# Attention, weight decoding and weight splitting without GpSimd arithmetic; phi in one VectorE instruction less a subtraction

## The chip, the cores and the metric

The kernel runs on one core of one Trainium2 chip. The metric is device microseconds of one execution, and a version's time is the median of its runs; less is better. The core's engines work beside each other, each through its own queue in order: TensorE (PE, with its weight loads as PEld), VectorE (DVE), ScalarE (ACT), GpSimd (POOL) and SyncE (SP, which issues the DMAs here).

## What is computed

Attention over 4 batches, 8 heads, 576 positions and 64 features, followed by two feed-forward layers of 2304 tokens, 512 columns and 2048 hidden columns. All inputs come as float64 words for the weights and float32 for the rest.

```python
scores = scale * q @ k.T, causal;  a = softmax(scores);  local = a @ v
phi(x) = where(x > 0, x, exp(x) - 1) + 1
mem_out = (phi(q) @ M_prev) / (phi(q) @ z_prev + 1e-6)
x = g * mem_out + (1 - g) * local          # g = sigmoid(beta), one number a head
h = x @ w_in;   x = gate(h) @ w_out        # first layer:  0, ((h + 1) ** 2) / 4 or h
h = x @ w2_in;  x = max(0.01 * h, h) @ w2_out
```

## The kernel before

Each float32 product is made of three products of float32r parts: a number is split into a high part (a cast) and a low part (the number less its high part). **Weights** take three steps. `load_raw` brings the float64 words of half a slot (128 hidden columns of W_in, or of W_out) as [128, 512, 2] integers. `decode_a` and `decode_b` make float32 of them: a ScalarE copy (L122), four VectorE instructions (L123, L127, L129, L130) and the addition L132 on GpSimd. `split` makes the two parts: a ScalarE copy (L188) and the subtraction L189 on GpSimd. There are 64 decoded halves in all, and 80 splits.

**Attention** goes by 16 units, each a pair of heads. `prep` splits and transposes q and k and makes phi: VectorE's minimum L297, GpSimd's q less the minimum (L298), ScalarE's exponential (L299), GpSimd's sum (L302), VectorE's row sum with z (L304 to L308) and GpSimd's product with the norm (L309). `scores` runs over five tiles of queries: matmuls, the masked minimum L360, the exponential L363, one over the sum (L365 to L367), and the product of e with it. That product is on VectorE (L370) for the first head of the first four tiles, and on GpSimd (L372) for the five others of a unit. `turn_a`, `turn_b` and `values` transpose e and multiply by v.

**Feed-forward.** Each layer is done in two halves of the hidden columns, each half over nine chunks of 256 tokens. A first-layer chunk has eight steps; a step is 12 matmuls (L527 to L529), ScalarE's L534 and L535, VectorE's L536 to L538, and, two steps later (`LAG`), 12 matmuls that use the result (L548 to L550). In the second layer a step has two slots: L576 to L578 for 24 matmuls, ScalarE's L581, VectorE's L582 to L586, ScalarE's L727, VectorE's L708, and 21 matmuls (L599 to L601) two such steps later. `finish2` adds up products on VectorE; when a chunk is visited the second time, L632 on GpSimd adds the first visit's part.

When one half of a layer gives way to the next, new weights have to be split into the places of the old ones. This happens at three **switches**: within the first layer (515 to 548 us of the trace), from the first to the second layer (740 to 783 us), and within the second layer (950 to 1000 us). The next weights are decoded ahead of that, at the steps in the tables `FETCH` and `HALVES`.

**Order.** While attention runs (the first 450 us), a scheduler sets each engine's order by its own estimate of times; the first-layer steps are interleaved by `target`. From then on every engine but SP goes in the order in which the code is written. An engine that waits holds all that stands behind it on its queue.

Of the kernel before, what the change touches and what calls it, by code (L numbers as in the profile page):

```python
# [25 lines left out]
# (layer, half of the hidden columns, chunks of tokens)  # L26
# [6 lines left out]
# whose quotients by the sums the vector engine works out: (tile of queries, head)  # L33
ON_DVE = {(i, 0) for i in range(4)}
# the tile of queries behind whose scores phi is transposed and v loaded
# [3 lines left out]
# tiles of scores between two of the first segment's slots, before the first, and from decoding to splitting  # L39
BOOT, BOOT0, DELAY = 2.0, 12.0, 1.0  # L40
# steps at which the next segment's weights are fetched
# [10 lines left out]
def attn_moe_moe_kernel(ctx, tc, q, k, v, m_prev, z_prev, beta, w1i, w1o, w2i, w2o, out):  # L52
# [17 lines left out]
    # scores are kept negated, so the mask is +1e9 and the row maximum is a minimum  # L70
# [4 lines left out]
    # both heads' last 64 queries stand one above the other  # L75
# [16 lines left out]
    # tiles with parts that are set once  # L92
# [5 lines left out]
    for s in range(2):  # L98
        # the last 64 queries: a head's own columns, zeros for the other head's
        ql = att.tile([128, 2, 128], F32R, bufs=1, name=f"ql{s}")  # L100
        nc.vector.tensor_copy(ql.rearrange("p a t -> p (a t)"), mask[:, 0:256])
        ql_t.append(ql)
        vn = att.tile([128, NKT, 2, D], F32, bufs=1, name=f"vn{s}")
        vn_t.append(vn)
# [21 lines left out]
    def decode_b(lo, dst, a, r):  # L126
# [5 lines left out]
        nc.gpsimd.tensor_tensor(dst, a.bitcast(F32), r, ALU.add)  # L132
# [3 lines left out]
    def l2_pool():  # L136
        """the second layer's tiles, in the attention's room"""
# [5 lines left out]
    def load_raw(seg, f, x):  # L143
        """a slot's float64 words of W_in (x = 0) or W_out (x = 1): [128, 512, 2]"""
# [18 lines left out]
    def fetch_halves(seg, halves):  # L163
        """weights as float32 in SBUF; two steps a half, the float64 words are loaded two halves ahead"""
# [22 lines left out]
    def split(dst, src):  # L187
        nc.scalar.activation(dst[:, 0], src, AF.Copy)  # L188
        nc.gpsimd.tensor_tensor(dst[:, 1], src, as_r(dst[:, 0]), ALU.subtract)  # L189
# [6 lines left out]
    def split_out(seg, p):  # L196
        """the second layer: W_out of two slots as the four blocks B and the combinations
        T1 = B12 - B11, T2 = B22 - T1, T3 = B22 - B12, T4 = T2 - B21; T1 takes the place of B12"""
# [20 lines left out]
    # a unit of attention: a pair of heads  # L219
# [21 lines left out]
    def prep(u):  # L241
        """-q/8 and k of a pair of heads, transposed, high part above low part, and phi of q over its norm"""
# [44 lines left out]
        # k with its parts exchanged, for the cross terms  # L287
# [5 lines left out]
        # phi(q) = exp(min(q, 0)) + (q - min(q, 0))  # L293
# [4 lines left out]
        nc.gpsimd.tensor_tensor(ph, qn, fe, ALU.subtract)  # L298
        nc.scalar.activation(fe, fe, AF.Exp)  # L299
        if u + 1 < len(UNITS):  # L300
            load_rows(q, qn, u + 1)
        nc.gpsimd.tensor_tensor(ph, ph, fe, ALU.add)  # L302
# [6 lines left out]
        nc.gpsimd.tensor_tensor(ph, ph, nn.unsqueeze(3).broadcast_to([128, NKT, 2, D]), ALU.mult)  # L309
# [18 lines left out]
    def scores(u, i):  # L328
        """exp of the scores less their maximum, over its sum and times the gate; of the last 64 rows, those of both
        heads at once"""  # L330
# [37 lines left out]
        for h, e in enumerate(es):  # L368
            if (i, h) in ON_DVE:
                nc.vector.tensor_scalar(out=e[:, 0:w], in0=e[:, 0:w], scalar1=ls[:, h:h + 1], scalar2=None, op0=ALU.mult)  # L370
            else:
                nc.gpsimd.tensor_tensor(e[:, 0:w], e[:, 0:w], ls[:, h:h + 1].broadcast_to([128, w]), ALU.mult)  # L372
        e_t[u, i] = es

    # the outputs of a pair of heads, features by queries: the first 256 queries, then the other 320
# [15 lines left out]
    def turn_b(u, j):  # L391
        """of the keys' tile j: first head: queries' tiles 2, 3 and 4; second head: 4, 2 and 3"""
# [23 lines left out]
    def values(u, half):  # L416
# [6 lines left out]
        for j, pt in enumerate(pts):  # L423
# [5 lines left out]
            else:  # L429
                # queries' tile 4 of the second head lies behind the first head's columns  # L430
# [11 lines left out]
    def attention_steps():  # L442
        """yields the number of tiles of 128 queries that are scored"""
# [65 lines left out]
    def load_prev(n):  # L509
        """what a chunk's first visit left"""  # L510
# [9 lines left out]
    def mm_h(n, f):  # L520
# [12 lines left out]
        # where h < 1: max(h / 2 + 1 / 2, 0) ** 2, at most 1; above: h  # L533
# [7 lines left out]
    def mm_y(n, f, yp, gg):  # L541
        w = slots[f, 1]
        gh, gl = gg
        for et in range(4):
            wh, wl = w[:, 0, 128 * et:128 * et + 128], w[:, 1, 128 * et:128 * et + 128]
            o = yp[et // 2][:, et % 2]
            # the two accumulators of a bank are one group
# [18 lines left out]
    def mm_h2(n, p):  # L566
        """lhsT blocks: 0 A21, 1 A11, 2 A22, 3 A12, 4 S1 = A21 + A22, 5 S2 = S1 - A11, 6 S3 = A11 - A21, 7 S4 = A12 - S2;
        A1. are the later 128 tokens of the chunk, A.1 the first slot"""
# [22 lines left out]
    def mm_y2(n, p, yp, gg):  # L591
        wa, wb, ex = slots["out", p]
        gh, gl = gg[1:]
        # P1 = A11 B11, P6 = S2 T2, P7 = S3 T3, P5 = S1 T1, P2 = A12 B21, P3 = S4 B22, P4 = A22 T4
        products = ((0, wa, 0), (4, ex, 0), (5, ex, 256), (3, wa, 256), (2, wb, 0), (6, wb, 256), (1, ex, 512))
        for i, (a, w, c) in enumerate(products):
            # the two accumulators of a bank are one group
# [5 lines left out]
    def finish2(n, yp):  # L603
# [15 lines left out]
        if last:  # L619
            # nothing runs beside it: the first visit's part goes into the summands that are ready early  # L620
# [182 lines left out]
```

## Time and profile before

| | us |
|---|---|
| median of three runs (lowest, highest) | 1178.47 (1175.47, 1181.21) |
| span of the profiled execution | 1174.2 |
| PE busy | 1085.9 (92%) |
| DVE busy | 949.5 (81%) |
| ACT busy | 583.5 (50%) |
| POOL busy | 389.0 (33%) |

The median is 4.3 us above the profiled execution's span; that execution's whole time is not listed apart. A matmul's busy time is longer than the distance to the next one's start, so that a PE that reads as fully busy may still not issue at its highest rate: the number of matmuls in a stretch tells more. The share of an engine over the whole span is a mean over stages that differ; the table of stretches below separates them. PEclk is the clock that TensorE was granted, as a share of the full one.

### The profile page before, as it was taken

What the parts mean: (1) busy time and instruction counts of PE and PEld (TensorE: products, weight loads), DVE (VectorE), ACT (ScalarE), POOL (GpSimd) and SP (SyncE); (2) the same over time, 40 slices, a digit from 0 to 9 for tenths busy, and PEclk for the clock granted to TensorE, in tenths of its full rate; (3) what the DMA queues carried; (4) which work ended last, traced back from release to release, by engine and by line L of the source; (5) the groups of instructions that cost most, each with busy time, mean ns of one, the idle gap of its engine ahead of it and who ended that gap; (6) DMA issues with size and microseconds to landing.
All of it is one profiled execution on the core that took longest, in us unless ns stands there. A gap on an engine that the chain in (4) does not pass through costs nothing.

```text
span 1174.2 us, 22682 instructions
## 1 busy us (share of the span) xinstructions
PE 1085.9 (92%) x8520; PEld 1023.8 (87%) x8520; DVE 949.5 (81%) x2125; ACT 583.5 (50%) x1314; POOL 389.0 (33%) x300
## 2 busy tenths in 40 slices
PE   5777687999999999997999999989999997999997
PEld 4544476999989889997999999889999997999997
DVE  5789999777677775998688787899999888876776
ACT  5755564766667765454333333444444444433332
POOL 3456666433343431236001111742121256211211
PEclk9866698999999999999999999989999998999999
DMA  5345444434334321432233433123232210121121
GB/s 146 93 97 144 139 128 132 111 80 125 102 76 116 77 60 60 142 108 72 80 119 122 130 114 121 55 72 127 90 103 96 91 37 37 63 100 55 66 79 55
DMA packets 122174, 112.11 MB, mean 95 GB/s; under 512 B 67280, under 2 KB 100048, under 8 KB 122064
## 3 DMA queue, kind: packets, MB, share of 16 engines
q1 hardware_dynamic: 122064, 110.66, 31.5%
q8 instruction: 67, 1.10, 0.4%
q14 instruction: 43, 0.35, 0.1%
HBM read 77.60 MB, written 23.59 MB: 86 GB/s over the span
## 4 chain that ended last, share of the span: by engine, by line
PE 68%; DVE 20%; issue 5%; POOL 3%; DMA 1%; ACT 1%; SPq 0%; DVEq 0%; POOLq 0%; ACTq 0%
PE A L576 5%; PE A L577 5%; PE A L578 5%; PE y L549 3%; PE A L527 3%; PE A L528 3%; PE A L529 3%; PE y L550 3%; PE A L348 3%; PE y L548 3%; PE y L601 3%; PE y L600 2%; PE y L599 2%; DVE gh L537 2%; DVE da L127 2%
## 5 line engine op out<-in xcount | busy, mean ns | idle before, releaser
L576 PE MATMUL A<-xh,i 128*128 128x256 f32 x576 | 163.7, 284 | 0.0
L577 PE MATMUL A<-xl,i 128*128 128x256 f32 x576 | 163.7, 284 | 0.0
L578 PE MATMUL A<-xh,i 128*128 128x256 f32 x576 | 163.5, 284 | 0.0
L132 POOL TENSOR_TENSOR w32b<-da,dr 128x512 f32<-128x512 f32 x36 | 55.2, 1532 | 282.2 <-DVE dr L130 269.3
L727 ACT ACTIVATE gh<-g 128x896 fp32r<-128x896 f32 x72 | 68.6, 953 | 155.9 <-DVE g L586 93.8
L363 ACT ACTIVATE e<-e,mx 128x128 f32<-128x128 f32 (+2 forms) x144 | 84.3, 586 | 76.3 <-DVE mx L360 72.7
L534 ACT ACTIVATE g<-A 128x256 f32<-128x256 f32 x98 | 37.6, 384 | 167.3 <-PE A L529 154.5
L372 POOL TENSOR_TENSOR e<-e,ls 128x128 f32<-128x128 f32 (+4 forms) x80 | 76.8, 960 | 123.6 <-DVE ls L367 59.3
L549 PE MATMUL y<-gl,o 128*128 128x256 f32 x384 | 112.2, 294 | 3.9 <-DVE gl L538 3.7
L548 PE MATMUL y<-gh,o 128*128 128x256 f32 x384 | 107.8, 289 | 5.7 <-DVE gh L537 5.7
L528 PE MATMUL A<-xl,i 128*128 128x256 f32 x392 | 111.3, 284 | 1.0 <-DVE xl L506 1.0
L527 PE MATMUL A<-xh,i 128*128 128x256 f32 x392 | 111.5, 284 | 0.0
L576 PEld LDWEIGHTS A<-xh,i 128*128 128x128 f32 x576 | 111.4, 193 | 0.0
L577 PEld LDWEIGHTS A<-xl,i 128*128 128x128 f32 x576 | 111.3, 193 | 0.0
L578 PEld LDWEIGHTS A<-xh,i 128*128 128x128 f32 x576 | 111.2, 193 | 0.0
L529 PE MATMUL A<-xh,i 128*128 128x256 f32 x392 | 111.2, 284 | 0.0
L550 PE MATMUL y<-gh,o 128*128 128x256 f32 x384 | 111.0, 290 | 0.0
L708 DVE TENSOR_TENSOR gl<-g,gh 128x896 fp32r<-128x896 f32 x72 | 87.8, 1219 | 19.8 <-ACT gh L727 19.8
L537 DVE CAST gh<-g 128x256 fp32r<-128x256 f32 x144 | 80.0, 556 | 19.6 <-PE y L550 7.9
L360 DVE CUSTOM_DVE_ANT_0 e<-A,mask 128x128 f32<-128x128 f32 (+4 forms) x126 | 59.6, 479 | 39.4 <-PE A L348 38.3
L549 PEld LDWEIGHTS y<-gl,o 128*128 128x128 f32 x384 | 74.7, 195 | 5.8 <-DVE gl L538 5.3
L548 PEld LDWEIGHTS y<-gh,o 128*128 128x128 f32 x384 | 72.9, 193 | 7.1 <-DVE gh L537 6.8
(289 smaller groups left out, 3736.8 us busy)
## 6 DMA issues: line engine op xcount, KB each, us to landing
raw<-in_moe_w_in_dram SPq DMA_DIRECT2D x32, 512.0 KB, 3.7
raw<-in_moe_w_out_dram SPq DMA_DIRECT2D x32, 512.0 KB, 3.3
qk<-qk SPq DMA_DIRECT2D x64, 144.0 KB, 2.4
xf<-y_d SPq DMA_DIRECT2D x18, 512.0 KB, 3.6
xf<-x_d SPq DMA_DIRECT2D x12, 512.0 KB, 4.0
yp_d<-ys SPq DMA_DIRECT2D x18, 256.0 KB, 2.3
xf<-yp_d SPq DMA_DIRECT2D x9, 512.0 KB, 3.2
y_d<-ys SPq DMA_DIRECT2D x18, 256.0 KB, 2.2
```

The lines of the kernel that those rows point to most:

```text
L363: nc.scalar.activation(e[:, 0:w], e[:, 0:w], AF.Exp, bias=mx, scale=-1.0, accum_out=ls[:, h:h + 1])
L527: nc.tensor.matmul(hp, wh, xh[:, ct], start=(ct == 0), stop=False)
L528: nc.tensor.matmul(hp, wh, xl[:, ct], start=False, stop=False)
L529: nc.tensor.matmul(hp, wl, xh[:, ct], start=False, stop=(ct == 3))
L537: nc.vector.tensor_copy(gh, g)
L548: nc.tensor.matmul(o, wh, gh, start=(f == 0 and et % 2 == 0), stop=False)
L549: nc.tensor.matmul(o, wh, gl, start=False, stop=False)
L550: nc.tensor.matmul(o, wl, gh, start=False, stop=(f == NSLOT - 1 and et % 2 == 1))
L576: nc.tensor.matmul(o, wh, xh[:, ct], start=(s == 0 and ct == 0), stop=False)
L577: nc.tensor.matmul(o, wh, xl[:, ct], start=False, stop=False)
L578: nc.tensor.matmul(o, wl, xh[:, ct], start=False, stop=(s == 1 and ct == 3))
L708: nc.vector.tensor_tensor(gl, g[:, 1:8], as_r(gh), ALU.subtract)
```

## The change

All GpSimd arithmetic of attention, decoding and splitting becomes VectorE arithmetic: L132 and L189 change their engine, L372 becomes the same per-row product as L370, and L309 changes its engine. Phi is now exp(min(q, 0)) + max(q, 0): L298 goes, and L302 becomes one VectorE instruction that takes the maximum of q and 0 and adds the exponential; it stands right behind the exponential. GpSimd keeps the fills at the start and the 16 additions of L632. Comments went too, so lines of the changed kernel have numbers up to six less.

```diff
-        nc.gpsimd.tensor_tensor(dst, a.bitcast(F32), r, ALU.add)
+        nc.vector.tensor_tensor(dst, a.bitcast(F32), r, ALU.add)
...
         nc.scalar.activation(dst[:, 0], src, AF.Copy)
-        nc.gpsimd.tensor_tensor(dst[:, 1], src, as_r(dst[:, 0]), ALU.subtract)
+        nc.vector.tensor_tensor(dst[:, 1], src, as_r(dst[:, 0]), ALU.subtract)
...
         nc.vector.tensor_scalar(out=fe, in0=qn, scalar1=0.0, scalar2=None, op0=ALU.min)
-        nc.gpsimd.tensor_tensor(ph, qn, fe, ALU.subtract)
         nc.scalar.activation(fe, fe, AF.Exp)
+        nc.vector.scalar_tensor_tensor(out=ph, in0=qn, scalar=0.0, in1=fe, op0=ALU.max, op1=ALU.add)
         if u + 1 < len(UNITS):
             load_rows(q, qn, u + 1)
-        nc.gpsimd.tensor_tensor(ph, ph, fe, ALU.add)
...
-        nc.gpsimd.tensor_tensor(ph, ph, nn.unsqueeze(3).broadcast_to([128, NKT, 2, D]), ALU.mult)
+        nc.vector.tensor_tensor(ph, ph, nn.unsqueeze(3).broadcast_to([128, NKT, 2, D]), ALU.mult)
...
-            if (i, h) in ON_DVE:
-                nc.vector.tensor_scalar(out=e[:, 0:w], in0=e[:, 0:w], scalar1=ls[:, h:h + 1], scalar2=None, op0=ALU.mult)
-            else:
-                nc.gpsimd.tensor_tensor(e[:, 0:w], e[:, 0:w], ls[:, h:h + 1].broadcast_to([128, w]), ALU.mult)
+            nc.vector.tensor_scalar(out=e[:, 0:w], in0=e[:, 0:w], scalar1=ls[:, h:h + 1], scalar2=None, op0=ALU.mult)
```

**First switch.** VectorE's queue in a step of the first layer at the first switch. Here da, dr and raw are decoding, g, gh and gl a step's result, i_ and o_ the split weights. Before:

```order
L123 TENSOR_SCALAR da<-raw 128x512
L127 SCALAR_TENSOR_TENSOR da<-w32b,da 128x512
L129 TENSOR_SCALAR dr<-da 128x512
L130 SCALAR_TENSOR_TENSOR dr<-raw,dr 128x512
L536 SCALAR_TENSOR_TENSOR g<-A,g 128x256
L537 CAST gh<-g 128x256
L538 TENSOR_TENSOR gl<-g,gh 128x256
```

The same step in the changed kernel:

```order
L187 TENSOR_TENSOR o_6954<-w_5026,o_6954 128x512
L187 TENSOR_TENSOR i_6957<-w_5464,i_6957 128x512
L121 TENSOR_SCALAR da<-raw 128x512
L125 SCALAR_TENSOR_TENSOR da<-w32b,da 128x512
L127 TENSOR_SCALAR dr<-da 128x512
L128 SCALAR_TENSOR_TENSOR dr<-raw,dr 128x512
L130 TENSOR_TENSOR w32b<-da,dr 128x512
L530 SCALAR_TENSOR_TENSOR g<-A,g 128x256
L531 CAST gh<-g 128x256
L532 TENSOR_TENSOR gl<-g,gh 128x256
```

Two split subtractions and the decoding's addition now stand ahead of the step's own three instructions.

**Third switch.** VectorE's queue in a step of the second layer at the third switch. Before, from the combinations of W_out to the next step's first instruction:

```order
L203 TENSOR_TENSOR g<-w32b 128x256
L204 TENSOR_TENSOR t<-w32b,g 128x256
L205 TENSOR_TENSOR t<-w32b 128x256
L206 TENSOR_TENSOR t<-t,w32b 128x256
L708 TENSOR_TENSOR gl_12406<-g_12398,gh_12405 128x896
L582 TENSOR_TENSOR g_12480<-A,g_12480 128x512
```

The same stretch of the changed kernel:

```order
L201 TENSOR_TENSOR g<-w32b 128x256
L202 TENSOR_TENSOR t<-w32b,g 128x256
L203 TENSOR_TENSOR t<-w32b 128x256
L204 TENSOR_TENSOR t<-t,w32b 128x256
L187 TENSOR_TENSOR wa<-w32b,wa 128x256
L187 TENSOR_TENSOR wb<-w32b,wb 128x512
L187 TENSOR_TENSOR i_12426<-w32b,i_12426 128x512
L187 TENSOR_TENSOR i_12429<-w32b,i_12429 128x512
L702 TENSOR_TENSOR gl_12390<-g_12382,gh_12389 128x896
L187 TENSOR_TENSOR wa<-g,wa 128x256
L187 TENSOR_TENSOR ex<-t,ex 128x768
L576 TENSOR_TENSOR g_12464<-A,g_12464 128x512
```

Four split subtractions now stand ahead of the low part gl, and two more behind it.

## Rows read from the trace of the kernel before

**Rows 1.** Stretches: us; busy us (xcount) of PE, PEld, DVE, ACT, POOL; clock; DMA.
```profile
70.00:212.00 142.00, 104.18 (x610) 81.48 (x612) 138.98 (x299) 82.03 (x214) 93.22 (x69) 0.76 0.47 132
212.00:515.00 303.00, 300.68 (x2474) 277.52 (x2469) 225.75 (x666) 192.66 (x526) 100.21 (x86) 1.00 0.35 96
515.00:548.00 33.00, 26.42 (x185) 25.13 (x186) 31.32 (x40) 16.47 (x34) 22.50 (x16) 0.90 0.26 80
548.00:740.00 192.00, 192.00 (x1602) 192.00 (x1602) 148.59 (x297) 65.63 (x157) 25.90 (x20) 1.00 0.34 110
740.00:783.00 43.00, 36.59 (x264) 35.58 (x263) 38.51 (x54) 20.41 (x39) 29.85 (x22) 0.88 0.16 54
783.00:950.00 167.00, 166.04 (x1384) 165.84 (x1383) 153.98 (x314) 75.09 (x105) 34.26 (x18) 1.00 0.29 97
950.00:1000.00 50.00, 41.94 (x331) 41.34 (x330) 41.72 (x68) 23.06 (x40) 30.62 (x23) 0.93 0.11 40
```

**Rows 2.** Timeline near 512 us: start, us, engine, line, what [idle before].
```profile
512.36 1.28 POOL L132 TENSOR_TENSOR w32b<-da,dr 128x512 f32<-128x512 f32 x1 [6.13 <-DVE dr L130]
...
512.66 1.14 DVE L537 CAST gh<-g 128x256 fp32r<-128x256 f32 x1
```

**Rows 3.** Three VectorE lines over the run: nanoseconds min/median/max.
```profile
L370 DVE TENSOR_SCALAR e<-e,ls x64: 220/420/1434, 18.0 to 443.2; 128x128 f32<-128x128 f32 x16, 128x256 f32<-128x256 f32 x16, 128x384 f32<-128x384 f32 x16, 128x512 f32<-128x512 f32 x16
...
L537 DVE CAST gh<-g x144: 223/294/1619, 148.5 to 759.3; 128x256 fp32r<-128x256 f32 x144
...
L365 DVE TENSOR_SCALAR ls<-ls x80: 134/156/1502, 16.1 to 446.9; 128x2 f32<-128x2 f32 x64, 128x1 f32<-128x1 f32 x16
```

**Rows 4.** VectorE by line, 70 to 212 us: busy us, mean ns | idle before.
```profile
L127 DVE SCALAR_TENSOR_TENSOR da<-w,da 128x512 int32<-128x512 int32 x19 | 19.7, 1036 | 0.1
L370 DVE TENSOR_SCALAR e<-e,ls 128x256 f32<-128x256 f32 (+3 forms) x16 | 16.9, 1059 | 0.0
L130 DVE SCALAR_TENSOR_TENSOR dr<-raw,dr 128x512 f32<-128x512 uint32 x20 | 15.9, 794 | 0.0
...
L123 DVE TENSOR_SCALAR da<-raw 128x512 int32<-128x512 int32 x19 | 13.6, 714 | 2.1 <-DMA raw<-in_moe_w_in_dram 2.1
L129 DVE TENSOR_SCALAR dr<-da 128x512 int32<-128x512 int32 x19 | 12.6, 664 | 0.1
L365 DVE TENSOR_SCALAR ls<-ls 128x2 f32<-128x2 f32 (+1 forms) x20 | 7.6, 378 | 0.0
...
L537 DVE CAST gh<-g 128x256 fp32r<-128x256 f32 x8 | 6.7, 834 | 0.0
```

**Rows 5.** VectorE by line, 548 to 740 us, where GpSimd is mostly idle.
```profile
L130 DVE SCALAR_TENSOR_TENSOR dr<-raw,dr 128x512 f32<-128x512 uint32 x16 | 11.1, 692 | 0.6
...
L127 DVE SCALAR_TENSOR_TENSOR da<-w32b,da 128x512 int32<-128x512 int32 x12 | 8.3, 693 | 1.2
L129 DVE TENSOR_SCALAR dr<-da 128x512 int32<-128x512 int32 x16 | 6.8, 427 | 0.5
L123 DVE TENSOR_SCALAR da<-raw 128x512 int32<-128x512 int32 x16 | 6.7, 420 | 0.0
```

**Rows 6.** GpSimd by line, 70 to 212 us.
```profile
L132 POOL TENSOR_TENSOR w<-da,dr 128x512 f32<-128x512 f32 x20 | 28.8, 1442 | 36.9 <-DVE ls L367 19.2 <-DVE dr L130 10.8 <-DVE ls L366 5.6
L372 POOL TENSOR_TENSOR e<-e,ls 128x256 f32<-128x256 f32 (+4 forms) x21 | 21.9, 1046 | 10.5 <-DVE ls L367 8.7 <-DVE ls L366 0.8 <-DVE ls L365 0.4
```

**Rows 7.** Line L189 alone in the stretches: us, GpSimd busy (instructions), clock, DMA.
```profile
70.00:212.00 142.00, 24.54 (x16) 0.76 0.47 132
515.00:548.00 33.00, 18.78 (x13) 0.90 0.26 80
740.00:783.00 43.00, 29.85 (x22) 0.88 0.16 54
950.00:1000.00 50.00, 30.62 (x23) 0.93 0.11 40
```

**Rows 8.** ScalarE's copy in a split, over the run.
```profile
L188 ACT ACTIVATE i<-w32b 128x512 fp32r<-128x512 f32 x17 | 9.9, 615 | 0.0
```

More of the change, by code (lines that the diff above doesn't have):

```diff
@@ L32 @@
 NW, RAWB, SPB, EB, GB = 4, 2, 2, (2, 2, 2, 2, 1), 2
-ON_DVE = {(i, 0) for i in range(4)}
 PHI, VL = 3, 0
```

## The prediction

> **What bounds the kernel now.** The table of stretches comes first, since an engine's share over the whole span mixes stages [rows 1]. In the second layer's quiet stretch PE issues 1384 matmuls in 167 us, in the first layer's 1602 in 192 us: 0.12 us each, with PE busy throughout. No work on another engine can shorten such a stretch. From 212 to 515 us, where attention ends beside the first layer, PE is busy for 300.7 of 303 us, which I read the same way. Four stretches are different. From 70 to 212 us VectorE is busy 139.0 of 142 us and PE 104, at a granted clock of 0.76: VectorE sets the pace. At the three switches PE issues 185, 264 and 331 matmuls, which at 0.12 us need 22.2, 31.7 and 39.7 us; the stretches last 33, 43 and 50 us. So 10.8, 11.3 and 10.3 us are lost there, 32.4 in all, and VectorE is busy 31.3 of 33, 38.5 of 43 and 41.7 of 50 us. Part of PE's loss is its clock, at 0.88 to 0.93 in these stretches: it fell after PE had waited and comes back with its work.
>
> Next I ask whether VectorE really works in that time. The cast L537 takes 0.29 us in the median and up to 1.62 [rows 3]. In the timeline one of 1.14 us starts 0.30 us after a GpSimd addition of 1.28 us and outlasts it by 0.16 us [rows 2]. Line by line the same instruction is long where GpSimd is busy (93 of 142 us) and short where it is mostly idle (26 of 192 us): L127 takes 1036 against 693 ns, L123 714 against 420, L129 664 against 427 [rows 1, 4, 5]. I read this as VectorE being held while GpSimd works. A good part of its busy time is waiting, and goes with GpSimd's instructions.
>
> **The change part by part: prices.** A moved addition or split subtraction of 512 columns does what L130 does, with two operands of that width: 0.69 us [rows 5]. A moved product with e is an L370: 0.42 us in the median of its four widths [rows 3]; the shape of 576 columns is a little wider. Phi's two instructions are 640 wide; no undisturbed row has this shape, so 0.69 scaled by the columns, an estimate of 0.87 us, lies between 0.69 and twice that. L298 costs nothing any more. The second layer's splits have 256, 512 and 768 columns; I price all at 0.69 us, which is dear for the narrow ones, more numerous than the wide.
>
> **Attention, 70 to 212 us.** Moved onto VectorE: 20 additions L132 and 16 subtractions L189, 36 times 0.69 = 24.8 us; 21 products L372, 21 times 0.42 = 8.8 us [rows 6, 7]. At five products a unit these are four units, with two phi instructions each: 8 times 0.87 = 7.0 us. Sum 40.6 us. Taken away, as count times (mean here less the undisturbed value): L127 19 x 343 ns = 6.5 us, L123 19 x 294 = 5.6, L129 19 x 237 = 4.5, L130 20 x 102 = 2.0, L370 16 x 639 = 10.2, L365 20 x 222 = 4.4, L537 8 x 540 = 4.3 [rows 3 to 5]. Sum 37.5 us from 121 of the stretch's 299 instructions. If the other 178 lost nothing, the stretch grows by 3 us. If a fifth of them, 36, lost the same 0.31 us each, 11 us more go and the stretch falls by 8. I take 5 us less: the splitting of q and k, phi and L367 are among the 178 and have the same kind of operands. Phi's chain also becomes shorter by two GpSimd instructions, but the start before 70 us hangs on loads and matmuls too; I count nothing there.
>
> **First switch.** VectorE has 40 instructions in 31.3 us, 0.78 us each; the same work from 548 to 740 us has 297 in 148.6, 0.50 each [rows 1]. The difference, 11.3 us, is a floor for what was waiting, since 0.50 holds some too. Added: 13 split subtractions and, by GpSimd's 16 instructions, 3 additions: 16 x 0.69 = 11.0 us [rows 1, 7]. VectorE would need 31.0 us. The gain lies between 2 us, if it still sets the pace and the floor is all, and 10.8 us, if PE does. A step's result is wanted two steps later, 24 matmuls or 2.9 us each, so VectorE may lag without stopping PE. I take 8 us, nearer to PE's end.
>
> **Second and third switch.** Second: 54 instructions at 0.71 us against 0.50 give 11.5 us; 22 subtractions add at most 15.2; VectorE 42.2 of 43 us; gain between 0.8 and 11.3 us, taken as 6. Third: 68 at 0.61 us against 0.49 (154.0 us by 314, 783 to 950 us) give 8.3 us; 23 subtractions add at most 15.9; VectorE 49.3 of 50; gain between 0.7 and 10.3 us, taken as 6 [rows 1, 7]. I go to the middle because the price is a ceiling, and because the delay of two steps covers a burst.
>
> **Where I cost it at nothing.** From 212 to 515, 548 to 740 and 783 to 950 us PE's matmuls hide VectorE. This cover is thin in the last: 154.0 of 167 us busy, and GpSimd's 18 instructions there become 12.4 us. Were nothing freed, VectorE would stand at 166.4 of 167 us, and bursts would cost some us. From 212 to 515 us 77 us are free, against GpSimd's 86 instructions of at most 0.87 us: 75 us. The additions L632, still on GpSimd, go on holding VectorE behind 1000 us, as now.
>
> **Waits that the move adds.** A split subtraction waits for ScalarE's copy of 0.62 us [rows 8]. On GpSimd this held up nobody; on VectorE the step's own g, gh and gl, or the second layer's gl, stand behind it, and PE wants those. At the first switch two copies a step are due behind the previous step's matmuls, while VectorE still decodes; mostly they will be done.
>
> **Sum.** 5 + 8 + 6 + 6 = 25 us off the span of 1174.2: 1149. The median shown is 4.3 us above that span, so the time is 1153 us.
>
> One rule speaks against the change. The Trainium skill, "Perfetto Trace Analysis", section "Optimizing Scalar/DVE Operations", says that where VectorE is saturated, moving work from it to ScalarE or even GpSimd may make sense, and adds that GpSimd shares an SBUF port with VectorE, so that moving between these two might not help. By its first half alone the moved 40.6 us would all be paid for (fourth rival); the 1036 against 693 ns of L127 agree with the second half. The Trainium skill, "SBUF — State Buffer", section "Who interferes with whom", has a VectorE instruction with two SBUF inputs, or in a two-port mode, blocked for the whole of a GpSimd instruction that reads SBUF; the timeline's 1.14 us cast agrees, and by that rule all excess goes.
>
> **The rivals.** *Deeper:* PE ends up the bound at all three switches and attention falls by its 8 us: 32.4 + 8 = 40 us, so 1138. For it: VectorE's floor is low. Against: VectorE's sum stays above PE's need in each switch. *No gain at the switches:* the floors are right, VectorE stays the bound there, 2.0 + 0.8 + 0.7 = 3.5 us, and attention loses 5 or gains 3: 1170 to 1178; 1173 in the middle. For it: all three sums come out within 2 us of the stretch. Against: the delay of two steps. *Slower by ScalarE's copies:* 74 of the split subtractions lie in the four stretches [rows 7]. If each held VectorE for a whole copy, 74 x 0.62 = 46 us, the time is 1153 + 46 = 1199. It cancels the gain from 0.34 us a piece, and shows as slower by over 0.5% (about 6 us, what a measurement here can tell from no change) from 0.42. For it: in the second layer ScalarE has four copies in a row, and VectorE only four short instructions to pass the time. Against: ScalarE is busy only 16.5 of 33, 20.4 of 43 and 23.1 of 50 us [rows 1]. *Slower, nothing is freed:* the long times are not GpSimd's doing. Then 40.6 + 11.0 + 15.2 + 15.9 = 83 us come onto an engine with 3.0 + 1.7 + 4.5 + 8.3 = 17.5 us free in these stretches: 66 us more, 1244. Against: every line in rows 4 and 5.
>
> **How the numbers follow.** Forecast 0.64 (1153, its own range 1143 to 1164), deeper 0.12 (1138), no gain at the switches 0.13 (1173), copies 0.07 (1199), nothing freed 0.04 (1244). Faster by over 0.5% (below 1172.6): 0.64 + 0.12 and half of the third case, 0.82. Within 0.5%: its other half, 0.07. Slower: 0.11. The range runs from 1136, a little past the deeper case, to 1175, past the third's middle; it leaves out some 0.05 below and 0.15 above.
>
> **What would show it.** Right: L127 near 0.69, L123 and L129 near 0.42, L370 near 0.42 us with no long ones, L537 at 0.29 throughout; VectorE's busy time about the same in total; the three switches shorter by 6 to 8 us each, the quiet stretches as long as now. Wrong: VectorE idle ahead of L187 with ScalarE's L186 as releaser (copies); long VectorE instructions with GpSimd idle (nothing freed); PE waiting for VectorE's gl between 783 and 950 us (thin cover).

## The result and the profile after

The changed kernel takes 1142.1 us (median of four runs, 1139.99 to 1144.17) against 1177.7 us (four runs, 1175.47 to 1181.21): a ratio of 0.9696, 95% interval 0.9673 to 0.9719, so 35.6 us less. The forecast was 1153 us, and its range 1136 to 1175. The sign, the mechanism and that range held. The narrower range of 1143 to 1164, to which the prediction gave a chance of 0.64, was missed by 1 us, because one of the terms of the 25 us, attention, was much too small.

To see where the 35 us went I follow the program by its feed-forward steps, not by the clock: step n begins with its first VectorE instruction (L536 before, L530 after; in the second layer, from step 144, L582 and L576). The times at which the two profiled executions reach a step:

| step | before, us | after, us | gained so far | in this stretch | forecast |
|---|---|---|---|---|---|
| 8, middle of attention | 211.9 | 182.8 | 29.1 | 29.1 | 5 |
| 48, attention over | 465.3 | 448.2 | 17.1 | -12.0 | 0 |
| 80, first switch over | 570.0 | 545.7 | 24.3 | 7.2 | 8 |
| 132 | 719.8 | 695.4 | 24.4 | 0.1 | 0 |
| 148, second switch over | 790.1 | 759.3 | 30.8 | 6.4 | 6 |
| 175 | 933.7 | 903.2 | 30.5 | -0.3 | 0 |
| 188, third switch over | 1014.8 | 979.3 | 35.5 | 5.0 | 6 |
| end of the span | 1174.2 | 1139.1 | 35.1 | -0.4 | 0 |

The three switches give 18.6 us (20 forecast), the quiet stretches nothing (0 forecast), attention 17.1 us (5 forecast, from 70 us on). Some of attention's gain is there by 70 us already: the 51st masked minimum of the scores (L357, before L360) starts at 65.1 us instead of 69.7. How much of that is the change is open: in the experiments below, with one or another of the moves, it starts between 64.6 and 71.0 us. The stretches of the kernel after, cut at these steps (busy us and instructions of PE, PEld, DVE, ACT, POOL, then clock, DMA share, GB/s), answer to [rows 1]:

```profile
70.00:182.80 112.80, 92.68 (x580) 75.00 (x580) 108.41 (x323) 74.44 (x193) 0.00 (x0) 0.79 0.53 148
182.80:448.20 265.40, 259.81 (x2097) 232.47 (x2096) 193.08 (x674) 175.60 (x494) 0.00 (x0) 0.99 0.35 90
448.20:545.70 97.50, 94.36 (x771) 92.64 (x770) 82.56 (x176) 45.22 (x99) 0.00 (x0) 1.00 0.33 108
545.70:695.40 149.70, 149.70 (x1250) 149.70 (x1249) 119.22 (x257) 50.14 (x119) 0.00 (x0) 1.00 0.39 121
695.40:759.30 63.90, 59.57 (x480) 58.97 (x480) 55.36 (x120) 30.51 (x61) 0.00 (x0) 0.97 0.23 75
759.30:903.20 143.90, 143.90 (x1201) 143.81 (x1200) 133.27 (x285) 64.01 (x88) 0.00 (x0) 1.00 0.32 106
903.20:979.30 76.10, 72.28 (x588) 71.84 (x587) 71.34 (x151) 37.41 (x60) 3.40 (x2) 0.98 0.15 50
```

The two cuts of attention and the three switches in the kernel before:

```profile
70.00:211.90 141.90, 104.08 (x609) 81.38 (x611) 138.88 (x297) 82.03 (x214) 93.12 (x69) 0.76 0.47 132
211.90:465.30 253.40, 252.34 (x2075) 229.58 (x2072) 180.13 (x582) 172.08 (x481) 88.69 (x77) 1.00 0.34 89
465.30:570.00 104.70, 96.86 (x770) 95.17 (x769) 88.54 (x148) 45.29 (x99) 36.70 (x27) 0.97 0.31 98
719.80:790.10 70.30, 63.89 (x491) 62.88 (x490) 61.23 (x93) 30.63 (x60) 35.75 (x26) 0.93 0.21 69
933.70:1014.80 81.10, 72.88 (x587) 72.07 (x586) 70.44 (x125) 37.52 (x60) 40.13 (x28) 0.96 0.13 47
```

By 70 us the changed kernel has done more of VectorE's work (169 instructions against 136), so attention's sums are taken from the start of the span to step 48, first before, then after:

```profile
0.00:465.30 465.30, 407.10 (x2973) 348.97 (x2974) 361.60 (x1013) 298.09 (x812) 207.20 (x177) 0.92 0.40 106
0.00:448.20 448.20, 401.59 (x2974) 342.74 (x2975) 349.96 (x1164) 296.28 (x811) 1.83 (x12) 0.94 0.42 109
```

VectorE has 151 instructions more and is 11.6 us less busy; its idle time fell from 103.7 to 98.2 us. PE's idle time fell from 58.2 to 46.6 us and its busy time, at a clock of 0.79 instead of 0.76 between 70 us and step 8, from 407.1 to 401.6 us; these 11.6 and 5.5 us are the 17.1.

The lines of VectorE from 70 to 183 us after the change (busy us, mean ns of one) answer to [rows 4]; L125, L121 and L127 are the former L127, L123 and L129, L128 the former L130, and L366 holds the former L370 and L372:

```profile
L366 DVE TENSOR_SCALAR e<-e,ls 128x256 f32<-128x256 f32 (+4 forms) x34 | 12.4, 400 | 0.0
...
L130 DVE TENSOR_TENSOR w<-da,dr 128x512 f32<-128x512 f32 x17 | 11.6, 684 | 0.0
L125 DVE SCALAR_TENSOR_TENSOR da<-w,da 128x512 int32<-128x512 int32 x16 | 10.9, 684 | 0.0
L128 DVE SCALAR_TENSOR_TENSOR dr<-raw,dr 128x512 f32<-128x512 uint32 x16 | 10.9, 680 | 0.0
L121 DVE TENSOR_SCALAR da<-raw 128x512 int32<-128x512 int32 x16 | 6.7, 420 | 1.9 <-DMA raw<-in_moe_w_out_dram 1.2 <-DMA raw<-in_moe_w_in_dram 0.7
L127 DVE TENSOR_SCALAR dr<-da 128x512 int32<-128x512 int32 x16 | 6.6, 413 | 0.0
L187 DVE TENSOR_TENSOR o<-w,o 128x512 fp32r<-128x512 f32 x8 | 5.5, 684 | 0.0
L187 DVE TENSOR_TENSOR i<-w,i 128x512 fp32r<-128x512 f32 x8 | 5.5, 684 | 0.9 <-ACT i L186 0.9
...
L297 DVE SCALAR_TENSOR_TENSOR ph<-qn,fe 128x640 f32<-128x640 f32 x3 | 2.4, 814 | 0.0
```

The four decoding lines' means are within 4% of what the lines had before where GpSimd was mostly idle [rows 5], L366's of its median before [rows 3] within 5%. Over the whole run (ns, least/median/most) the long ones of [rows 3] are gone; L531 is the former L537, L362 the former L365:

```profile
L531 DVE CAST gh<-g x144: 279/294/296, 128.7 to 731.7; 128x256 fp32r<-128x256 f32 x144
```
```profile
L366 DVE TENSOR_SCALAR e<-e,ls x144: 277/414/521, 17.8 to 434.1; 128x128 f32<-128x128 f32 x32, 128x256 f32<-128x256 f32 x32, 128x384 f32<-128x384 f32 x32, 128x512 f32<-128x512 f32 x32
```
```profile
L362 DVE TENSOR_SCALAR ls<-ls x80: 108/162/171, 16.8 to 433.5; 128x2 f32<-128x2 f32 x64, 128x1 f32<-128x1 f32 x16
```

Rows from the list of who waited for whom over the run (us in total, times, longest): PE's two longest waits behind attention, at the second and the third switch, and the largest of line L187's waits for a copy:

```profile
PE y L595 <- DVE gl L702: 4.2, 1, 4.2
...
PE h L593 <- DVE ys L620: 3.5, 1, 3.5
...
DVE i L187 <- ACT i L186: 1.4, 2, 0.9
```

The last row is the mark that I had named for the rival of ScalarE's copies: two waits of 1.4 us in all, and 0.5 us more for L187's other tiles.

### The profile page after: what moved, and what is told of

The parts are those of the page before. It is cut to its first block, busy times and chain, and to the rows that moved or that the text cites. A ratio compares the mean times of both kernels' runs of the same rounds, so it can differ in the third digit from the quotient of the medians.

```text
span 1139.1 us, 22315 instructions
## 1 busy us (share of the span) xinstructions
PE 1074.1 (94%) x8520; PEld 1012.2 (89%) x8520; DVE 926.5 (81%) x2382; ACT 581.6 (51%) x1313; POOL 29.0 (3%) x28
## 4 chain that ended last, share of the span: by engine, by line
PE 75%; DVE 13%; DMA 4%; ACT 2%; issue 1%; SPq 1%; DVEq 0%; ACTq 0%
PE A L570 6%; PE A L571 6%; PE A L572 6%; PE A L522 3%; PE A L521 3%; PE A L523 3%; PE y L543 3%; PE y L542 3%; PE y L544 3%; PE y L595 3%; PE y L594 3%; PE y L593 3%; PE A L345 3%; PE h L521 2%; PE A L426 2%; PE h L522 2%
## 5 line engine op out<-in xcount | busy, mean ns | idle before, releaser
L570 PEld LDWEIGHTS A<-xh,i 128*128 128x128 f32 x576 | 111.0, 193 | 0.0
L571 PEld LDWEIGHTS A<-xl,i 128*128 128x128 f32 x576 | 111.0, 193 | 0.0
L572 PEld LDWEIGHTS A<-xh,i 128*128 128x128 f32 x576 | 110.9, 193 | 0.0
L360 ACT ACTIVATE e<-e,mx 128x128 f32<-128x128 f32 (+2 forms) x144 | 84.0, 583 | 27.3 <-DVE mx L357 26.4
L357 DVE CUSTOM_DVE_ANT_0 e<-A,mask 128x128 f32<-128x128 f32 (+4 forms) x126 | 60.2, 481 | 42.6 <-PE A L345 41.2
L575 ACT ACTIVATE g<-A 128x512 f32<-128x512 f32 x72 | 42.7, 593 | 71.4 <-PE A L572 71.4
L522 PEld LDWEIGHTS A<-xl,i 128*128 128x128 f32 x392 | 75.3, 192 | 0.4 <-DVE xl L500 0.4
L521 PEld LDWEIGHTS A<-xh,i 128*128 128x128 f32 x392 | 75.3, 192 | 0.4 <-issue 0.4
```

The costliest lines, as they stand in the source:

```text
L360: nc.scalar.activation(e[:, 0:w], e[:, 0:w], AF.Exp, bias=mx, scale=-1.0, accum_out=ls[:, h:h + 1])
L521: nc.tensor.matmul(hp, wh, xh[:, ct], start=(ct == 0), stop=False)
L522: nc.tensor.matmul(hp, wh, xl[:, ct], start=False, stop=False)
L570: nc.tensor.matmul(o, wh, xh[:, ct], start=(s == 0 and ct == 0), stop=False)
L571: nc.tensor.matmul(o, wh, xl[:, ct], start=False, stop=False)
L572: nc.tensor.matmul(o, wl, xh[:, ct], start=False, stop=(s == 1 and ct == 3))
```

## The experiments

**Is it GpSimd's reading that holds VectorE?** The changed kernel with dead work on GpSimd: once additions and subtractions that read two operands, once fills that only write. They stand behind the addition and the split subtraction (the expectation of the fills says ahead of them), on tiles that nobody reads any more.

```diff
         nc.vector.tensor_tensor(dst, a.bitcast(F32), r, ALU.add)
+        nc.gpsimd.tensor_tensor(r, a.bitcast(F32), r, ALU.add)
...
         nc.vector.tensor_tensor(dst[:, 1], src, as_r(dst[:, 0]), ALU.subtract)
+        nc.gpsimd.tensor_tensor(src, src, as_r(dst[:, 0]), ALU.subtract)
```

> The changed kernel, in which GpSimd repeats each of the 64 decoding additions and 80 split subtractions into a tile that is dead by then; nobody waits for it except for the reuse of that tile. Theory (VectorE is held while a GpSimd instruction that reads SBUF runs): VectorE keeps the moved work and is held again; in the attention stretch 36 GpSimd instructions hold it for about 0.5 us each, 18 us, and the three switches lose 8 to 11 us each; 1142 + 18 + 27 = 1187, above the kernel before; the step's cast takes 0.8 us or more where GpSimd runs. Rival (the gain is the shorter chain: GpSimd's 1.5 us result came late): nobody waits for GpSimd, so 1142 as the changed kernel, and the cast stays at 0.29 us.

Measured: 1231.2 us (1228.5 to 1232.8), ratio to the kernel before 1.0456 (1.0432 to 1.0481): 89 us more than the changed kernel, although VectorE has the same instructions. The loss lies in attention (27 us) and at the switches (19, 19 and 22 us). In attention the scheduler also made another order of it, so its 27 us are not the holding's alone; behind step 48 VectorE's order is that of the changed kernel. The three switches, cut at the same steps:

```profile
475.60:592.50 116.90, 101.30 (x766) 96.98 (x765) 104.66 (x176) 45.07 (x98) 37.46 (x27) 0.96 0.28 88
743.70:827.00 83.30, 67.27 (x492) 65.08 (x492) 76.20 (x120) 30.84 (x60) 38.98 (x26) 0.88 0.18 59
973.90:1071.70 97.80, 77.77 (x584) 75.73 (x583) 92.96 (x153) 37.32 (x60) 46.34 (x28) 0.90 0.13 43
```

VectorE's busy time grew by 22.1, 20.8 and 21.6 us with the same work (82.56, 55.36 and 71.34 us above), and the stretches by 19.4, 19.4 and 21.7 us: here VectorE's held time is the kernel's time. The direction was as expected, the size twice it: I had expected 8 to 11 us a switch, but each GpSimd instruction held VectorE for 0.8 us (22.1 us by 27, 20.8 by 26, 21.6 by 28), and nearly all of that lay on the path, since VectorE now also has the moved work.

```diff
         nc.vector.tensor_tensor(dst, a.bitcast(F32), r, ALU.add)
+        for _ in range(3):
+            nc.gpsimd.memset(r, 0.0)
...
         nc.vector.tensor_tensor(dst[:, 1], src, as_r(dst[:, 0]), ALU.subtract)
+        for _ in range(3):
+            nc.gpsimd.memset(src, 0.0)
```

> The changed kernel, to which GpSimd adds three fills of the addition's tile ahead of each decoding addition and three of the source tile ahead of each split subtraction in the first layer and attention; they read nothing and the addition and the subtraction follow behind them in the same tile's order, so the output is the same. GpSimd gets some 480 short instructions and is busy about as often as with the repeated additions of the run before, but it only writes. Theory, that what holds VectorE is GpSimd reading: the cast stays at 0.29 us, L123's and L127's lines at 0.42 and 0.69, and the time is 1142 us, plus some us for the wait that the fills put before the next use of the tile, up to 1150. Rival, that any GpSimd instruction holds VectorE: the cast's mean goes to 0.5 us, and the time towards 1231 as in the run with repeated additions.

Measured: 1149.3 us (1146.3 to 1152.3), 0.9762 (0.9736 to 0.9787), with GpSimd busy for 261 us (251 in the run before). Two VectorE lines in the run that reads and in the one that only writes (ns, least/median/most): the cast, and the subtraction for gl, which reads two tiles of SBUF.

```profile
L533 DVE CAST gh<-g x144: 264/294/1370, 137.1 to 788.5; 128x256 fp32r<-128x256 f32 x144
```
```profile
L534 DVE TENSOR_TENSOR gl<-g,gh x144: 399/426/1942, 141.8 to 788.9; 128x256 fp32r<-128x256 f32 x144
```
```profile
L535 DVE CAST gh<-g x144: 278/294/727, 129.0 to 735.5; 128x256 fp32r<-128x256 f32 x144
```
```profile
L536 DVE TENSOR_TENSOR gl<-g,gh x144: 396/425/428, 131.8 to 736.1; 128x256 fp32r<-128x256 f32 x144
```

Beside reading GpSimd instructions both lines reach 1.4 to 1.9 us. Beside fills the subtraction is never held (428 ns at most), the cast still is, up to 727 ns: it ends 0.15 us behind a fill of 0.53 us that began 0.05 us after it. In this run VectorE, ScalarE and PE go in the changed kernel's order, so the two traces can be compared instruction by instruction: VectorE's durations add up to 13 us more, and the seven lines that gained over 0.5 us are all casts and tensor_scalar instructions, which have one operand of full width (5.2 us of it in the products with e). The theory stands for the two-operand instructions; for the one-operand ones it was too narrow. The 7 us above the changed kernel fit these 13, but no run shows them apart.

**Which of the moves pays?** Single moves taken back, with GpSimd's line as it was before the change.

```diff
-        nc.vector.tensor_tensor(dst, a.bitcast(F32), r, ALU.add)
+        nc.gpsimd.tensor_tensor(dst, a.bitcast(F32), r, ALU.add)
...
-        nc.vector.tensor_tensor(dst[:, 1], src, as_r(dst[:, 0]), ALU.subtract)
+        nc.gpsimd.tensor_tensor(dst[:, 1], src, as_r(dst[:, 0]), ALU.subtract)
```

> The changed kernel with decoding's additions and the split subtractions on GpSimd again. Theory: the switches go back to their old length, 7 + 6.5 + 4.6 = 18 us, and the attention loses the 36 instructions' share of its 17 us, about 9: 1169. Rival (attention's own arithmetic brought the 17 us): 1160. Rival (it is all one sum, and half the work gives half): 1160 with switches shorter than before.

Measured: 1165.9 us (1162.0 to 1167.9), 0.9895 (0.9864 to 0.9927). Attention keeps 10.9 us of the gain, the switches nothing. That is between the theory's 1169 us and the 1160 of its rivals, and nearer to the theory, which had the switches right.

The second of these two edits alone:

> The changed kernel with the 80 split subtractions alone on GpSimd again. Theory: the switches are made by the splits, 58 of them there against 3 additions, so they return to their old length, 18 us, and the attention loses its 16 subtractions' share, 4 us: 1164. Rival (decoding's additions hold VectorE as much): 1152.

Measured: 1158.2 us (1156.3 to 1164.8), 0.9848 (0.9813 to 0.9884). Attention keeps all (18.1 us), where I had expected 4 us less, and the switches lose nearly all of theirs (1.6 us left). The cast has its long ones again, one at 134 us and the others at the first two switches:

```profile
L531 DVE CAST gh<-g x144: 277/294/1440, 133.9 to 739.5; 128x256 fp32r<-128x256 f32 x144
```

So the split subtractions make nearly the whole gain at the switches and none of attention's; the decoding additions, taken back together with the splits, make 18.1 - 10.9 = 7.2 us of attention's. In the next run attention's own arithmetic is back on GpSimd, phi's three instructions and the five products a unit:

```diff
+        nc.gpsimd.tensor_tensor(ph, qn, fe, ALU.subtract)
         nc.scalar.activation(fe, fe, AF.Exp)
-        nc.vector.scalar_tensor_tensor(out=ph, in0=qn, scalar=0.0, in1=fe, op0=ALU.max, op1=ALU.add)
...
+        nc.gpsimd.tensor_tensor(ph, ph, fe, ALU.add)
...
-        nc.vector.tensor_tensor(ph, ph, nn.unsqueeze(3).broadcast_to([128, NKT, 2, D]), ALU.mult)
+        nc.gpsimd.tensor_tensor(ph, ph, nn.unsqueeze(3).broadcast_to([128, NKT, 2, D]), ALU.mult)
...
-            nc.vector.tensor_scalar(out=e[:, 0:w], in0=e[:, 0:w], scalar1=ls[:, h:h + 1], scalar2=None, op0=ALU.mult)
+            if i < 4 and h == 0:
+                nc.vector.tensor_scalar(out=e[:, 0:w], in0=e[:, 0:w], scalar1=ls[:, h:h + 1], scalar2=None, op0=ALU.mult)
+            else:
+                nc.gpsimd.tensor_tensor(e[:, 0:w], e[:, 0:w], ls[:, h:h + 1].broadcast_to([128, w]), ALU.mult)
```

> The changed kernel with phi and the products with e on GpSimd again, decoding and splitting on VectorE. Theory: the three switches stay as short as in the changed kernel, and the attention gives back the share of its 29 instructions, 8 us: 1150. Rival (attention's arithmetic is what mattered there): 1159. Rival (only the sum of VectorE's work counts, and GpSimd relieves it): faster than 1142.

Measured: 1153.0 us (1152.5 to 1153.7), 0.9795 (0.9776 to 0.9814). Attention keeps 4.6 us, the switches all of their gain; the time lies between the theory's 1150 us and the first rival's 1159. Then the last hunk of that diff alone (80 of the 144 products; the 112 in the expectation is a miscount):

> The changed kernel with the 112 products with e back on GpSimd as before the change; phi, the decoding additions and the split subtractions stay on VectorE. With all of attention's arithmetic back the time was 1153.0 us, 10.9 more than the changed kernel. Theory, that GpSimd's long instructions hold VectorE's in proportion to their number (112 products against two phi subtractions, additions and products a tile): most of it goes with the products, 1149 to 1152 us, with the switches as short as in the changed kernel. Rival, that phi's chain at the head of each unit is what counts: 1142 to 1146 us.

Measured: 1142.9 us (1139.2 to 1144.9), 0.9698 (0.9672 to 0.9725), the changed kernel's time. The rival was right: the products pay nothing, phi pays the difference between these two runs, 10.1 us. Attention in both, from the start to step 48, and GpSimd's lines in it (count, busy us and mean ns), first with all of it back:

```profile
0.00:460.70 460.70, 406.68 (x2973) 347.02 (x2974) 363.29 (x1054) 296.63 (x809) 155.73 (x140) 0.93 0.41 106
```
```profile
L370 POOL TENSOR_TENSOR e<-e,ls 128x128 f32<-128x128 f32 (+4 forms) x80 | 78.1, 977 | 196.7 <-DVE ls L365 101.3 <-DVE nn L304 21.5 <-ACT sp L257 12.0
...
L300 POOL TENSOR_TENSOR ph<-ph,fe 128x640 f32<-128x640 f32 x16 | 26.6, 1664 | 2.6 <-ACT fe L297 2.5
L296 POOL TENSOR_TENSOR ph<-qn,fe 128x640 f32<-128x640 f32 x16 | 25.6, 1598 | 60.2 <-PE A L319 49.8 <-DVE fe L295 6.0 <-DMA qk<-qk 4.4
L307 POOL TENSOR_TENSOR ph<-ph,nn 128x640 f32<-128x640 f32 x16 | 24.4, 1524 | 32.3 <-DVE nn L306 15.0 <-DVE ls L365 11.8 <-DVE ls L364 5.5
```

and with the products alone:

```profile
0.00:450.40 450.40, 401.06 (x2973) 343.83 (x2974) 348.83 (x1078) 298.25 (x816) 74.86 (x92) 0.94 0.42 109
```

Taking the 48 long phi instructions off GpSimd and putting 32 on VectorE leaves VectorE with 24 more instructions and 14.5 us less busy; seven copies, which the scheduler may put on either engine, went to ScalarE at that. Taking the 80 products off as well (the changed kernel: 1164 instructions in 350.0 us) gives VectorE 86 more instructions and 1.1 us more: what they held and what they cost are about even.

**Why does attention give 12 us back behind step 8?** Three runs around the middle of attention. In the first the next x is loaded one slot earlier, with VectorE's and PE's order as they were. The edit acts while attention runs, and not once it is over, as the expectation has it:

```diff
-                if f == (3 if attended else 5):
+                if f == (3 if attended else 4):
```

> The changed kernel with the load of the next x after slot 4 instead of slot 5 in the first layer once attention is over, nothing else moved but for its place on SP. Theory, that attention ends only 17 us earlier although step 8 comes 29 us earlier because PE sets the pace behind step 8 and not because of x's loads: no change, 1142 us, within 2 us. Rival, that late x loads (7.7 us of waits ahead of the split of x, over the whole kernel) give some of the gain back: 4 to 7 us less, 1135 to 1138.

Measured: 1141.3 us (1137.3 to 1144.2), 0.9689 (0.9665 to 0.9713). The waits for x shrank by 1.4 us, from 7.7 to

```profile
DVE xh L493 <- DMA xf<-x_d: 6.3, 4, 2.9
```

and the time not measurably: x isn't what gives the gain back. This run reaches step 8 at 188.3 us (182.8 in the changed kernel) and step 48 at 450.3 us (448.2) with the same order, so one execution's place of step 8 is uncertain by some 5 us, the end of attention by 2.

```diff
-    marks = [(0, 20.0), (5, 24.0), (13, 44.0), (29, 64.0), (45, 86.0)]
+    marks = [(0, 21.0), (5, 25.0), (13, 45.0), (29, 65.0), (45, 86.0)]
```

> The changed kernel with the table that paces the first layer's steps against attention's moved by 1, so that more of attention stands ahead of the first steps. Theory, that the order decides how much VectorE work stands ahead of step 8 but PE's total work decides when attention ends: step 8 comes some 5 to 8 us later than in the changed kernel, attention ends within 3 us of it, 1139 to 1145 us. Rival, that the gain in attention is the order's doing (work put behind step 8): step 8 and the end of attention move together, by 5 to 10 us, 1147 to 1152.

Measured: 1143.7 us (1143.1 to 1144.9), 0.9715 (0.9697 to 0.9734). Step 8 at 190.0, attention over at 450.8 us: step 8 is 7 us later than in the changed kernel (2 later than in the run with the earlier x), the end of attention hardly at all. That is a small shift beside the 5 us of doubt, but the run with the products back shows the same with a larger one: step 8 at 196.2 us, attention over at 450.4, and the changed kernel's time. How far the first steps are pushed ahead into attention doesn't decide the time.

```diff
         for h, e in enumerate(es):
+            if h == 1 and u < 6:
+                nc.scalar.activation(e[:, 0:w], e[:, 0:w], AF.Identity, scale=ls[:, h:h + 1])
+                continue
```

> The changed kernel with the e products of the second head of the first six units (24 of 144) on ScalarE instead of VectorE. ScalarE is busy 75 of 113 us from 70 to 183 us, VectorE 109. Theory, that VectorE sets the pace there: about 15 of the 24 lie in that stretch, at 0.42 us each 6 us off VectorE, and step 8 comes 4 to 6 us earlier; most of it is given back behind, where PE sets the pace, so 1138 to 1142 us. Rival, that the chain through ScalarE sets it: a product there is longer, step 8 comes no earlier or later, 1142 to 1150.

Measured: 1143.0 us (1138.0 to 1146.0), 0.9704 (0.9675 to 0.9732), step 8 at 188.5 us. With work taken from VectorE nothing became earlier, so the theory that VectorE's sum alone still sets the pace there has no support from this run; that ScalarE's longer way cost what VectorE gained is as possible.

**Is there more to have?** In the changed kernel PE's longest gap behind attention is at 744 us. The timeline (start, us, engine, line, [idle before]):

```profile
742.18 0.42 DVE L187 TENSOR_TENSOR wa<-w,wa 128x256 fp32r<-128x256 f32 x1
...
742.51 0.68 DVE L187 TENSOR_TENSOR wb<-w,wb 128x512 fp32r<-128x512 f32 x1
...
743.11 1.08 DVE L702 TENSOR_TENSOR gl<-g,gh 128x896 fp32r<-128x896 f32 x1
...
744.25 0.39 PE L595 MATMUL y<-wa,gl 128*128 128x256 f32 x1 [4.18 <-DVE gl L702]
```

PE waits for gl, and gl stands behind the step's split work on VectorE. So I put it ahead:

```diff
+                low_part(*gg)
                 do_jobs(x)
-                low_part(*gg)
```

> The changed kernel with the second layer's subtraction for gl put ahead of the step's split work on VectorE instead of behind it. In the changed kernel PE's longest gaps behind attention are 4.2 us at 744 us, ahead of a matmul that waits for gl, behind four split subtractions, and 3.5 us at 946 us. Theory, that a split subtraction queued ahead of gl is what PE waits for: the gap at 744 us shrinks to about 1 us, 2 to 4 us less at the second switch and as much at most at the third, 1136 to 1140 us. Rival, that the split subtractions' own results are wanted next and VectorE's sum sets the pace there: the gap moves on to a matmul that waits for a split, 1141 to 1144 us.

Measured: 1158.1 us (1153.9 to 1160.9), 0.9826 (0.9799 to 0.9853): 16 us slower, where I expected 2 to 6 faster. The gap at 744 us is gone, but the second switch as a whole is no shorter (64.3 against 63.9 us), and the quiet stretch behind it takes 152.5 instead of 143.9 us, the third switch 80.8 instead of 76.1. The timeline at one quiet step:

```profile
787.86 0.29 DVE L580 TENSOR_TENSOR g<-g 128x128 f32<-128x128 f32 x1
789.25 1.09 DVE L702 TENSOR_TENSOR gl<-g,gh 128x896 fp32r<-128x896 f32 x1 [1.10 <-ACT gh L721]
790.26 0.69 DVE L125 SCALAR_TENSOR_TENSOR da<-w32b,da 128x512 int32<-128x512 int32 x1
```

The same wait over the run, here and in the changed kernel (us, times, longest):

```profile
DVE gl L702 <- ACT gh L721: 40.9, 37, 1.4
```
```profile
DVE gl L702 <- ACT gh L721: 19.8, 18, 1.1
```

gl needs ScalarE's copy gh. In the changed kernel the split and decoding work fills that time; with gl ahead VectorE stands still and the work comes later, and with it the additions of `finish2` (L620), which PE waits for ten times instead of once (3.5 us in the rows above):

```profile
PE h L593 <- DVE ys L620: 11.2, 10, 2.7
```

Two last runs put L626's additions on VectorE, once with gl ahead and once alone:

```diff
-                    nc.gpsimd.tensor_tensor(t, t, pp[:, 512 * i:512 * i + 512], ALU.add)
+                    nc.vector.tensor_tensor(t, t, pp[:, 512 * i:512 * i + 512], ALU.add)
```

> The changed kernel with the subtraction for gl ahead of the split work, as in the other run, and the last 16 additions on VectorE too instead of GpSimd, which then does nothing behind the start. Theory, that the quiet stretch behind 962 us belongs to PE (170 of 177 us busy) and hides these additions on either engine: the same as the run with gl ahead alone, within 2 us. Rival, that they hold VectorE where PE waits for it: 2 to 4 us less than that run.

> The changed kernel with the last 16 additions on VectorE instead of GpSimd, nothing else. By the same theory no change, 1140 to 1144 us; by the rival 1138 to 1140.

Measured: 1157.2 us (1153.5 to 1158.3) with gl ahead and 1141.7 us (1139.6 to 1143.7), 0.9692 (0.9666 to 0.9717), alone. Neither differs measurably from its partner: behind 979 us PE is busy for 152.7 of 159.8 us, and that hides the additions on either engine. The theory of both runs held. No run beat the changed kernel measurably.

## Why the prediction was right, and where it was off

**The bound and the mechanism** held. VectorE was held by GpSimd: the decoding lines came out at the undisturbed prices of [rows 5], the same instructions became long again with dead GpSimd work, and 151 more instructions up to the end of attention left VectorE 11.6 us less busy. I also took each VectorE instruction of the kernel before between 70 and 500 us and subtracted the median of the same line and shape after: the 369 with a GpSimd instruction beside them had lost 75 us, the 569 without one nothing (-1.7 us). The rule of the Trainium skill, "SBUF — State Buffer", section "Who interferes with whom", which I had weighed, goes on to say that a VectorE instruction with two SBUF inputs contends with a GpSimd instruction that reads SBUF and not with one that only writes it, while the two-port modes, which a cast can enter, contend with GpSimd without that condition. The fills agree with both halves: the subtraction 428 ns at most, the cast 727. The other rule of the Trainium skill, from "Perfetto Trace Analysis", section "Optimizing Scalar/DVE Operations", had two halves; the runs bear out the second, that work given from VectorE to GpSimd might not help VectorE: taking it back relieved it.

**The switches** were sized rightly: 8, 6 and 6 us forecast, 7.2, 6.4 and 5.0 measured. That they agree within 1 us is partly luck, since 8 and 6 were picked between wide bounds. By the comparison above, VectorE was held for 14.0, 16.7 and 12.5 us in the three stretches of the prediction, whose floors were 11.3, 11.5 and 8.3: the floors were indeed low. In the cuts above VectorE's busy time fell by 6.0 and 5.9 us at the first two switches, close to the gain, and rose by 0.9 us at the third, where its idle time fell from 10.7 to 4.8 us. So VectorE stayed near its limit (71.3 of 76.1 us in the third) and PE's end was not reached. With the split subtractions back on GpSimd 1.6 of the 18.6 us are left, so the cause is the one named.

**The quiet stretches** stayed as long as they were (149.7 for 149.8, 143.9 for 143.6 us), as costed at nothing. The cover that I called thin held: VectorE is busy for 133.3 of 143.9 us there, 1.7 more than before for 13 more instructions.

**Attention** is the term that was mis-sized: 5 us forecast, between +8 and -3, and 17.1 measured, outside these ends. The prices were right: 684 ns for 690, 400 for 420, 814 for 870. Three things were not. First, what was to be freed: I took 45.6 us from 121 instructions and a share of the rest; the instructions of before from 70 us to step 8, at the means of after, give 49. Second, what was added there: 34.7 us instead of 40.6, and some 13 us of VectorE's older work lies elsewhere, since the scheduler orders attention anew: by 70 us 58 of L357's instructions are done (51 before), and by step 8 only 17 halves have been decoded (20 before). I had treated the stretch as a fixed load that the change adds to. What went behind step 8 is no gain by itself: PE is busy there, and 12 us were given back; the runs with later marks and with the products back say the same. Third, and the largest by the runs, the parts: phi is worth 10 us, the additions 7, the products and the split subtractions in attention nothing, each uncertain by some 2 us. On phi the prediction said that its chain becomes shorter by two GpSimd instructions, and that it counts nothing there; it had only the time ahead of 70 us in mind. That term, put at nothing, is where attention's sum failed most. In the unit's chain three GpSimd instructions of 1.5 to 1.7 us became two of VectorE of 0.81.

**What stays open** is how phi's 10 us divide between the shorter chain and VectorE's freed time. By durations phi's instructions held VectorE for some 24 us between 70 and 500 us of the kernel before, against 26 instructions at 0.81 = 21 us added, 3 us net; the products 16.5 us against 69 at 0.40 = 28, a loss of 11. Measured were 10 and about 0: phi comes out 7 us better and the products 11 us better than the sum of durations. That two queued instructions take less than their durations (below) explains some of it: from the start to step 48 VectorE's durations add up to 419.7 us before and 428.4 after, 9 us more, while its busy time fell by 11.6. The chain may explain the rest; no run took the two apart. The additions' 7 us are open in the same way: ScalarE's split copies waited for GpSimd's additions for 15.4 us in the kernel before (L188 for L132), and for VectorE's for 3.3 us after (L186 for L130).

**The rivals.** Deeper (1138) had 8 us for attention, still too little, and PE's bound at all switches, which didn't come; its time is only 4 us from the result, and by luck: 9 us too little in attention stand against 14 too much at the switches. No gain at the switches (whose middle of 1170 to 1178 is 1174, not 1173) fell with 18.6 us of gain there. Nothing freed fell with the casts. The copies: 1.9 us of waits where 46 were feared; the copies are mostly done when VectorE comes to them. The run with gl ahead shows that the mechanism itself is real: with 21 us more of such waits the kernel took 16 us more, when the work that stood between the copy and its reader was taken away.

## What to carry to other kernels

Where VectorE looks busy, compare the same line's duration in stretches with GpSimd active and idle; if it differs, GpSimd's work may be cheaper on VectorE than beside it, and the price of the move is the undisturbed one. Work out the gain for each moved group by itself and ask which chain it stands in: here split subtractions paid at the switches alone, phi and the decoding additions in attention alone, and 80 products not at all. Add up busy time rather than durations where instructions stand queued. On an engine that goes in order, work between a copy and its reader is a cover; putting the reader first can turn it into a wait.

## What the hardware showed

- A GpSimd fill, which reads nothing, lengthens VectorE's cast from 294 to as much as 727 ns, but not a subtraction with two SBUF operands (425 ns in the median, 428 at most). GpSimd arithmetic lengthens both, to as much as 1370 and 1942 ns.
- Instructions as small as 128x2 were held as long as a whole GpSimd instruction: 1502 ns at most in [rows 3], 171 after.
- Queued VectorE instructions can begin before the one ahead has ended by the trace, so a duration is not the price. In the changed kernel (start, us):

```profile
726.64 0.42 DVE L187 TENSOR_TENSOR wa<-w32b,wa 128x256 fp32r<-128x256 f32 x1
726.98 0.68 DVE L187 TENSOR_TENSOR wb<-w32b,wb 128x512 fp32r<-128x512 f32 x1
727.58 1.28 DVE L187 TENSOR_TENSOR i<-w32b,i 128x512 fp32r<-128x512 f32 x2
```

  0.42 us of duration take 0.34, and 0.68 take 0.60: 0.08 us less each. For the 65 instructions of my 40.6 us that is up to 5 us too dear.
